# A planned attention-and-mixer kernel: z turned by overlapping twos of tiles, more buffers, shared homes for turned blocks, later projections

## The chip, the cores and the metric

One NeuronCore of a Trainium2 chip runs the whole kernel. Its engines are TensorE (PE, matmuls; PEld are its weight loads), VectorE (DVE), ScalarE (ACT), GpSimd (POOL) and SyncE (SP, which here only issues DMAs). The metric is device time in microseconds (us) of one launch; less is better.

## The reference

Eight batches of 3200 tokens; `u`, `v` have 256 columns, `z` has 64, the weights are 256 x 64 (`w_q`, `w_k`) and 256 x 256 (`w_out`). All is given and returned in float32.

```python
# gated attention
scores = matmul(z, z.transpose(0, 2, 1)) / S
attn = maximum(scores, 0.0) ** 2
x = u * matmul(attn, v)
# token mixer without softmax
wq, wk = x @ w_q, x @ w_k
W_tok = einsum('bsd,btd->bst', wq, wk) / sqrt(64)
mixed = einsum('bst,btd->bsd', W_tok, x)
out = maximum(mixed, 0.0) @ w_out
```

## The kernel before

**Tiling.** A batch's 3200 tokens are 25 tiles of 128 rows (`NT`), in seven groups: six of 512 rows and a last one of 128 (`widths`, `starts`, `LASTG`). For each group of columns `gi` the kernel forms scores against tiles `ti` of rows: one matmul of 64 x 128 by 64 x 512. Since z has 64 columns, half the rows of the array are enough for one tile; two tiles run side by side on the upper and the lower half. So z^T has to stand twice, in partitions 0 to 63 and again in 64 to 127.

**Stages.** `use_pair` (line 632) takes one of two PSUM slots, calls `scores` (242) for a pair of tiles, and gives the eviction max(., 0) times a constant to ScalarE or VectorE (`first_stage`, 262). `squares` (650) gives the square, in float16, to ScalarE or GpSimd (`second_stage`, 279); it lands in one of `NAT` = 14 buffers `at`. Scores are symmetric, so a block computed for group `gi` also serves group `gj` if it is transposed: `turn` (304) does this with a DMA transpose issued by SyncE, for groups at a distance of 1 or 2 and for the last group (`is_turned`, 212). Turned blocks live in tiles `tt1` (three), `tt2` (four) and `ttl` (eight). `second_product` (326) accumulates block times v into four PSUM banks (two halves of the group, two halves of the array). When a half is complete, `gate` (342) copies one bank on ScalarE, adds the other on VectorE and multiplies with u on GpSimd: that is `x_sb`, `NX` = 6 buffers. Later `turn_x` (380) transposes x by DMA, `projections` (397) forms queries and keys, `turn_keys` (416) transposes these, `double_keys` (426) copies them on GpSimd, `heads` (433) accumulates the small matrix keys^T x, and `mix` and `proj` (462, 485) form the output.

**z.** For the first batch, z is loaded in four pieces, doubled by casts into `zd0` and transposed on TensorE. For each later batch, `load_z` (154) loads z in float16 through GpSimd's DMA queue to `zn`; `double_z` (158) copies it twice on VectorE, so that each 128-column block of `zd` holds one tile's 64 columns two times; and `turn_z` (163) makes five DMA transposes of five blocks each into `zT`.

**What sets the order.** The program is written out by a planner. It keeps a clock for each engine with fixed costs, and at each step chooses the next piece of work for TensorE: a pair of scores, an extra (`keys`, `heads`, `mix`, `proj`) or the next step of the second product (loop at 963). SyncE's DMAs wait in `moves`, each with a time from which it may go and a due time; the earliest due goes first (`flush`, 598). A pair may be computed only when all readers of its `at` buffer have been planned and its transposes have landed (line 981). `XWAIT` (818) holds the projections back after x has been turned; `z_here` (803) holds scores of a batch until its last turn of z has landed in the plan. On the chip the engines run in the order so written, each held by semaphores.

Of the kernel before, what the change touches and what calls it, by code (L numbers as in the profile page):

```python
# [16 lines left out]
def kernel(  # L17
# [10 lines left out]
    nc = tc.nc  # L28
# [20 lines left out]
    ALPHA = C1 * float(S) * float(S)  # L49
    FINAL_SCALE = 1.0 / (8.0 * ALPHA * ALPHA * ALPHA)  # L50

    NAT = 14
    NX = 6
    NEARBY = 8
    KEEP = 4

# [6 lines left out]
    pxt = ctx.enter_context(tc.tile_pool(name="pxt", bufs=3))  # L63
# [18 lines left out]
    def top(r):  # L82
        return slice(r * dqk, (r + 1) * dqk)

    ctx.enter_context(tc.manual_schedule())

    zT, vs, us, xs, xTs, qks, ks, hacc, hss, rts, zds = ({} for _ in range(11))

    def rows(t, b):
        return t[b].rearrange("(p n) d -> p n d", n=NT)  # L90
# [6 lines left out]
    zd0 = pz.tile([P, NT, 2, dqk], FP16, tag="zd", name="zd")  # L97
    vs[0] = pv.tile([P, NT, D], FP16, tag="v_sb", name="v_sb")
    zT[0] = pzt.tile([P, S], FP16, tag="zT2", name="zT2")

    def load_first_z():
        for i, (n0, nn) in enumerate(ZCH):
# [49 lines left out]
    zdense, ztimes = {}, []  # L152

    def load_z(b):
        zdense[b] = pz.tile([P, NT, dqk], FP16, tag="zn", name="zn")
        nc.gpsimd.dma_start(out=zdense[b][:], in_=rows(z, b))

    def double_z(b, half):
        if half == 0:
            zds[b] = pz.tile([P, NT, 2, dqk], FP16, tag="zd", name="zd")  # L160
        nc.vector.tensor_copy(out=zds[b][:, :, half, :], in_=zdense[b][:])

    def turn_z(b, i):
        ztimes.append((b, i))
        if i == 0:
            zT[b] = pzt.tile([P, S], FP16, tag="zT2", name="zT2")
        nc.sync.dma_start_transpose(
            out=zT[b][:].rearrange("p (n s) -> p n s", s=P)[:, 5 * i : 5 * i + 5, :],
            in_=zds[b][:, 5 * i : 5 * i + 5, :, :].rearrange("p n a k -> p (n a k)"),
        )  # L170

    def load_u(b, gi):
        n0, nn = starts[gi] // P, widths[gi] // P
# [2 lines left out]

    wq32 = consts.tile([P, NC, dh], FP32, tag="wq32", name="wq32")
    wk32 = consts.tile([P, NC, dh], FP32, tag="wk32", name="wk32")  # L180
# [27 lines left out]


    SKIP = [(0, 2)]  # L210

    def is_turned(b, gi, gj):
        if b == 0 and (gi, gj) in SKIP:
            return False
        return gi < gj and (gj <= gi + FAR or gj == LASTG)

    def group_of(ti):
# [20 lines left out]
    NTILE = len(tiles)  # L238
    NPAIR = NTILE // 2
    made, turned = {}, {}  # L240

    def scores(p):
        assert len(ztimes) >= 5 * tiles[2 * p + 1][0] and p_chunk(p) in z_at, (p, clock, len(ztimes), z_at)
        sc = ps_tile("sc")
        for h, (b, gi, ti) in enumerate(tiles[2 * p : 2 * p + 2]):
            gs, gw = starts[gi], widths[gi]
            nc.tensor.matmul(  # L247
                out=sc[:, h, 0:gw],
                lhsT=zT[b][top(h), ts(ti, P)],
                rhs=zT[b][top(h), ds(gs, gw)],  # L250
                start=True,
                stop=True,
            )
        return sc
# [24 lines left out]
    def second_stage(p, g, ways):  # L279
        at = pat.tile([P, 2 * W], FP16, tag="at", name="at")  # L280
        at0 = 0
        parts = pieces(p)
        if len(ways) > len(parts):
            parts = [(slice(h, h + 1), parts[0][1]) for h in range(2)]
        for (hs, w), on_act in zip(parts, ways * 2):
            n = hs.stop - hs.start
            out = at[:, at0 : at0 + n * w].rearrange("p (n w) -> p n w", w=w)
            if on_act:
                nc.scalar.square(out=out, in_=g[:, hs, 0:w])  # L289
            else:  # L290
                nc.gpsimd.tensor_mul(out=out, in0=g[:, hs, 0:w], in1=g[:, hs, 0:w])  # L291
# [12 lines left out]
        def turn(b, gi, gj, n0, nn, c0, c1):  # L304
            if (b, gi, gj) not in turned:
                kind, nr, bufs = ("l", 1, 8) if gj == LASTG else (gj - gi, 4, gj - gi + 2)
                turned[b, gi, gj] = ptt.tile(
                    [P, nr, 4, P], FP16, tag=f"tt{kind}", name=f"tt{kind}", bufs=bufs
                )
# [32 lines left out]
    def gate(b, gi, half):  # L342
# [8 lines left out]
        )  # L351
        if b == last and gi >= LASTG - 2:
            if gi == LASTG - 2 and half == 0:
                spare = pz.tile([P, NT, 2, dqk], FP16, tag="zd", name="xd")
                spare = spare[:].rearrange("p n a k -> p (n a k)")
                spare = spare[:, 0 : 9 * D].rearrange("p (n d) -> p n d", d=D)
# [21 lines left out]
        make_x()  # L378

    def turn_x(b, gi):  # L380
        assert len(xTs) < 3
# [236 lines left out]
    def cold():  # L618
        return 2.0 if clock[PE] < 8.4 else 1.0

    SPLIT = 0.2
    UNTIL = 24.0

# [26 lines left out]
    def squares():  # L650
        while pending and pending[0][0] <= clock[PE] + 0.3:
# [8 lines left out]
                done = give(ACT, ready, 1.06) if on_act else give(POOL, ready, 1.9)  # L660
            for (b, gi, gj, _, nn, _, _), turn in second_stage(p, g, ways):
                n = nn * widths[gi] // P
                due = done + (4.0 if gj == gi + 1 else 9.0)
                out_of[p] = out_of.get(p, 0) + 1
                move(done + SLACK, due + SLACK, 1.28, 0.21 * n, turn, lambda t, x=(p, b, gi, gj, nn): block_landed(t, *x))
            for x in tiles[2 * p : 2 * p + 2]:
                row_at[x] = done + 0.6

# [100 lines left out]
        dma_at[0] = max(dma_at[0], clock[PE]) + takes  # L769

    Z0 = 24
    V0 = 56
    V1 = 11

    def batch_begun(b, t):
        if b + 1 < B:
            t0 = max(t + 6, Z0)
            at_time(t0, lambda: (load_z(b + 1), push(3.0)))
            for half in range(2):
                at_time(  # L780
                    t0 + 12 + 3 * half,
                    lambda half=half: (double_z(b + 1, half), give(DVE, clock[PE], 0.98)),
                )
# [18 lines left out]

    def z_here(p):
        b = tiles[2 * p + 1][0]
        return not b or z_ready.get((b, 4), 1e9) <= clock[PE]

    def group_begun(b, gi, t):
        if gi == 0:
# [6 lines left out]
    SPARE = 0.3  # L815
    BIAS = 0.2
    XDUE = 5.0
    XWAIT = 3.0
    LATE = 0.3

    last_x = []
# [1 line left out]
    def half_done(b, gi, half):  # L823
# [8 lines left out]
        if make_x:  # L832
            last_x.append(make_x)
        elif half == halves(gi)[-1]:
            n = 8 if widths[gi] == W else 2
            move(
                t + SLACK, t + XDUE, 1.28, 0.21 * n, lambda: turn_x(b, gi),
                lambda t: x_landed(t, b, gi), lambda: len(xTs) < 3,
            )

    def x_landed(t, b, gi):
# [52 lines left out]
    def acc_step():  # L894
# [6 lines left out]
        fn()  # L901
        clock[PE] += 0.1093 * cold()
        used.add(row)
        if closes:
            half_done(b, gi, half)
        return True
# [191 lines left out]
```

## Time and profile before

| what | value |
|---|---|
| three plain times | 783.07, 788.03, 788.28 us (median 788.03) |
| profiled execution | 784.44 us, of which the span from first to last instruction is 782.7 us |
| DMA transposes of squares (`tt`), of the last group (`ttl`) | 143 and 48, 4.3 and 3.7 us from issue to landing |
| DMA transposes of x, of keys, of z | 56, 53 and 35; 5.8, 4.1 and 4.8 us |
| loads of z after the first batch | 7 of 400 KB, 6.8 us |
| DMA queue of SyncE | 82.1% of the 16 DMA engines' span |

All spans, waits and counts are of the one profiled execution. Busy time of TensorE includes the filling of its pipeline: a matmul of 256 columns is shown as 269 ns, while the next may start after some 107.

### The profile page before, as it was taken

What the parts mean: (1) busy time and instruction counts of PE and PEld (TensorE: products, weight loads), DVE (VectorE), ACT (ScalarE), POOL (GpSimd) and SP (SyncE); (2) the same over time, 40 slices, a digit from 0 to 9 for tenths busy, and PEclk for the clock granted to TensorE, in tenths of its full rate; (3) what the DMA queues carried; (4) which work ended last, traced back from release to release, by engine and by line L of the source; (5) the groups of instructions that cost most, each with busy time, mean ns of one, the idle gap of its engine ahead of it and who ended that gap; (6) DMA issues with size and microseconds to landing.
All of it is one profiled execution on the core that took longest, in us unless ns stands there. A gap on an engine that the chain in (4) does not pass through costs nothing.

```text
span 782.7 us, 28343 instructions
## 1 busy us (share of the span) xinstructions
PE 769.8 (98%) x12410; PEld 663.7 (85%) x12410; DVE 503.3 (64%) x515; ACT 546.4 (70%) x663; POOL 645.1 (82%) x530
## 2 busy tenths in 40 slices
PE   7999999999999999999999999999999999999996
PEld 5899999788899878888889887998889888898784
DVE  6766556655587556786476665777567556566635
ACT  6868777668676767766677767776678676777534
POOL 7898988788889877888789889778788879888961
PEclk9999999999999999999999999999999999999999
DMA  7999999999999999999799989999999998969635
GB/s 179 143 174 170 157 181 180 165 175 206 216 174 177 211 184 189 185 212 189 180 177 174 220 173 201 168 164 217 190 188 152 183 228 166 202 127 210 142 59 213
DMA packets 306300, 140.88 MB, mean 180 GB/s; under 512 B 285056, under 2 KB 287744, under 8 KB 306176
## 3 DMA queue, kind: packets, MB, share of 16 engines
q1 hardware_dynamic: 299408, 122.90, 82.1%
q0 software_dynamic: 6624, 15.98, 15.0%
q8 instruction: 97, 1.59, 0.9%
q10 hardware_dynamic: 144, 0.20, 0.1%
q14 instruction: 27, 0.22, 0.1%
HBM read 59.64 MB, written 26.21 MB: 110 GB/s over the span
## 4 chain that ended last, share of the span: by engine, by line
PE 92%; DVE 2%; DMA 1%; ACT 1%; POOL 1%; issue 1%; DVEq 0%; SPq 0%; ACTq 0%
PE acc L332 67%; PE sc L247 13%; PE fo L493 6%; PE qk L401 3%; PE qk L438 2%; PE mx L466 1%; DVE g L273 1%; DMA v_sb<-in_v_dram 1%; POOL at L291 1%; ACT g L269 1%; ACT at L289 0%; DMA z<-in_z_dram 0%; DVE fo L516 0%; PE hd L438 0%; DVE both L349 0%
## 5 line engine op out<-in xcount | busy, mean ns | idle before, releaser
L291 POOL TENSOR_TENSOR at<-g 128x1024 f16<-128x1024 f32 (+2 forms) x252 | 457.1, 1827 | 62.4 <-DVE g L273 50.3
L332 PE MATMUL acc<-v_sb,at 64*128 64x256 f16 x7344 | 498.4, 269 | 1.2 <-DMA v_sb<-in_v_dram 0.7
L273 DVE TENSOR_SCALAR g<-sc 128x1024 f32<-128x1024 f32 (+2 forms) x320 | 372.6, 1178 | 135.3 <-PE sc L247 126.7
L332 PEld LDWEIGHTS <-at 64*128 64x128 f16 x7344 | 400.9, 94 | 55.2 <-issue 8.1
L289 ACT ACTIVATE at<-g 128x1024 f16<-128x1024 f32 (+2 forms) x230 | 228.1, 1008 | 19.2 <-DVE g L273 17.0
L269 ACT ACTIVATE g<-sc 128x1024 f32<-128x1024 f32 (+2 forms) x159 | 156.5, 986 | 67.1 <-PE sc L247 58.5
L247 PE MATMUL sc<-zT 64*128 64x512 f16 x924 | 187.6, 377 | 1.9 <-DVE g L273 0.8
L370 POOL TENSOR_TENSOR x_sb<-both,u_sb 128x512 f16<-128x512 f32 (+1 forms) x112 | 134.7, 1209 | 43.9 <-DVE both L349 43.6
L332 PE MATMUL acc<-v_sb,tt 64*128 64x256 f16 x2272 | 159.2, 269 | 0.0
L332 PEld LDWEIGHTS <-tt 64*128 64x128 f16 x2272 | 123.5, 94 | 14.3
L349 DVE TENSOR_TENSOR both<-acc,both 128x512 f32<-128x512 f32 (+1 forms) x104 | 69.7, 670 | 86.4 <-ACT both L348 73.3
L348 ACT COPY both<-acc 128x512 f32<-128x512 f32 (+1 forms) x104 | 59.0, 568 | 70.7 <-PE acc L332 66.4
L247 PEld LDWEIGHTS <-zT 64*128 64x128 f16 x924 | 60.8, 94 | 12.9 <-issue 8.9
L521 ACT ACTIVATE fo<-fo 128x1024 f32<-128x1024 f32 (+1 forms) x48 | 44.6, 930 | 24.3 <-PE fo L493 23.8
L493 PE MATMUL fo<-wo,rt 128*128 128x256 f16 x400 | 53.2, 274 | 1.3 <-ACT rt L481 0.5
L483 ACT ACTIVATE rt<-mx 128x1024 f16<-128x1024 f32 (+1 forms) x49 | 45.6, 934 | 11.5 <-PE mx L466 11.2
L414 ACT CAST qk<-qk 128x512 f16<-128x512 f32 (+1 forms) x54 | 29.4, 544 | 30.0 <-PE qk L438 24.1
L493 PEld LDWEIGHTS <-rt 128*128 128x128 f16 x400 | 34.9, 98 | 15.8 <-issue 10.9
L453 DVE TENSOR_TENSOR ha<-qk,ha 128x512 f32<-128x512 f32 x37 | 25.6, 691 | 30.7 <-ACT qk L414 30.2
L401 PE MATMUL qk<-xT_sb,wqk 64*128 64x256 f16 (+1 forms) x404 | 32.4, 265 | 0.0
L431 POOL COPY kx<-kx 128x128 f16<-128x128 f16 (+1 forms) x99 | 26.2, 294 | 5.7 <-DMA kx<-qk 5.7
L438 PE MATMUL qk<-x_sb,kx 64*128 64x256 f16 x342 | 28.4, 269 | 0.0
(45 smaller groups left out, 233.7 us busy)
## 6 DMA issues: line engine op xcount, KB each, us to landing
u_sb<-in_u_dram SPq DMA_DIRECT2D x48, 512.0 KB, 4.9
out_dram<-fo SPq DMA_DIRECT2D x47, 512.0 KB, 5.2
v_sb<-in_v_dram POOLq DMA_DIRECT2D x35, 320.0 KB, 5.5
zn<-in_z_dram POOLq DMA_DIRECT2D x7, 400.0 KB, 6.8
tt<-at SPq DMA_TRANSPOSE x143, 4.3
u_sb<-in_u_dram SPq DMA_DIRECT2D x8, 128.0 KB, 3.1
out_dram<-fo SPq DMA_DIRECT2D x8, 128.0 KB, 3.4
xT_sb<-x_sb SPq DMA_TRANSPOSE x56, 5.8
```

Of the source, the lines that this page charges most:

```text
L247: nc.tensor.matmul(out=sc[:, h, 0:gw], lhsT=zT[b][top(h), ts(ti, P)], rhs=zT[b][top(h), ds(gs, gw)], start=True, stop=True,)
L269: nc.scalar.activation(out=g[:, hs, 0:w], in_=sc[:, hs, 0:w], func=RELU, scale=GSCALE)
L273: nc.vector.tensor_scalar(out=g[:, hs, 0:w], in0=sc[:, hs, 0:w], scalar1=0.0, scalar2=GSCALE, op0=AOP.max, op1=AOP.mult,)
L289: nc.scalar.square(out=out, in_=g[:, hs, 0:w])
L291: nc.gpsimd.tensor_mul(out=out, in0=g[:, hs, 0:w], in1=g[:, hs, 0:w])
L332: nc.tensor.matmul(out=accs[half, r][:, ds((j % 2) * D, D)], lhsT=weights(b, gi, ti, j)[top(r), :], rhs=vs[b][top(r), ti, :], start=(first ...
L348: nc.scalar.copy(out=both[:, 0 : n * D], in_=accs[half, 0][:, 0 : n * D])
L349: nc.vector.tensor_add(out=both[:, 0 : n * D], in0=accs[half, 1][:, 0 : n * D], in1=both[:, 0 : n * D])
L370: nc.gpsimd.tensor_mul(out=xs[b, gi][:, 0:n, :, r, :].rearrange("p n c d -> p (n c) d"), in0=both[:, 0 : n * D].rearrange("p (m d) -> p m ...
L401: nc.tensor.matmul(out=ps[:, r, 0 : n * P], lhsT=wqk[top(r), c, :, :].rearrange("p t h -> p (t h)"), rhs=xTs[b, gi][top(r), 0:n, c, :], st ...
L483: nc.scalar.activation(out=out, in_=ps[:, 0:nr, 0 : ND * n * P], func=RELU)
L493: nc.tensor.matmul(out=banks[r][:, ds(j * D, D)], lhsT=flat[:, ds((dc * n + j) * P, P)], rhs=wo[:, dc, :], start=(dc == 0 and j == 0), sto ...
```

## The change

- z of the later batches isn't copied any more. `zn` becomes one tile of 27 blocks of 64 columns: a zero block, the 25 tiles, a zero block. A transpose of two neighbouring blocks gives 128 rows: the left tile above, the right tile below. All overlapping twos are turned (blocks 0 and 1, 1 and 2, up to 25 and 26), the even ones in two DMAs of seven and six, the odd ones likewise. In `zT` each tile then stands below in its own column block, and above one block further right, so `zT` has 128 more columns and `z_cols` shifts the upper half's reads.
- The turns may go from 14 us after the load in the plan, in steps of 7 (5 in the first batch), instead of from 18 in steps of 6 (4).
- `NAT` goes from 14 to 16, `NX` from 6 to 7, the buffers of turned x from 3 to 4 (`NXT`).
- Blocks at a distance of 1 or 2 share seven homes, which are handed out and given back in the plan; a turn without a free home waits (`has_home`). Their due time is 4 us at distance 1, 9 at 2, and 12 for the last group's farther blocks.
- `XWAIT` goes from 3 to 7.
- The first batch's doubled z, and the last batch's x, use a buffer of v; the first weights use one of the output buffers. `EXTRA` is empty.

```diff
-    NAT = 14
-    NX = 6
+    NAT = 16
+    NX = 7
+    NXT = 4
...
     def load_z(b):
-        zdense[b] = pz.tile([P, NT, dqk], FP16, tag="zn", name="zn")
-        nc.gpsimd.dma_start(out=zdense[b][:], in_=rows(z, b))
-
-    def double_z(b, half):
-        if half == 0:
-            zds[b] = pz.tile([P, NT, 2, dqk], FP16, tag="zd", name="zd")
-        nc.vector.tensor_copy(out=zds[b][:, :, half, :], in_=zdense[b][:])
+        nc.gpsimd.dma_start(out=zn[:, 1 : NT + 1, :], in_=rows(z, b))
 
     def turn_z(b, i):
+        odd, m0, m1 = ZTURNS[i]
         ztimes.append((b, i))
         if i == 0:
-            zT[b] = pzt.tile([P, S], FP16, tag="zT2", name="zT2")
+            zT[b] = pzt.tile([P, S + P], FP16, tag="zT2", name="zT2")
         nc.sync.dma_start_transpose(
-            out=zT[b][:].rearrange("p (n s) -> p n s", s=P)[:, 5 * i : 5 * i + 5, :],
-            in_=zds[b][:, 5 * i : 5 * i + 5, :, :].rearrange("p n a k -> p (n a k)"),
+            out=zT[b][:].rearrange("p (m o s) -> p o m s", o=2, s=P)[:, odd, m0:m1, :],
+            in_=zn[:, 2 * m0 + odd : 2 * m1 + odd, :].rearrange("p n k -> p (n k)"),
         )
+
+    def z_cols(b, h, at, n):
+        return zT[b][top(h), ds(at + (P if b and h == 0 else 0), n)]
...
+    NHOME = 7
+    homes, homes_free = {}, list(range(NHOME))
+
+    def has_home(b, gi, gj):
+        return gj == LASTG or (b, gi, gj) in turned or bool(homes_free)
+
+    def give_home_back(b, gj, t):
+        gi = group_of(t)
+        if (b, gi, gj) in homes and all(
+            (b, gj, starts[gi] // P + n) in used for n in range(widths[gi] // P)
+        ):
+            homes_free.append(homes.pop((b, gi, gj)))
...
-                lhsT=zT[b][top(h), ts(ti, P)],
-                rhs=zT[b][top(h), ds(gs, gw)],
+                lhsT=z_cols(b, h, ti * P, P),
+                rhs=z_cols(b, h, gs, gw),
...
-                due = done + (4.0 if gj == gi + 1 else 9.0)
+                due = done + {1: 4.0, 2: 9.0}.get(gj - gi, FARDUE)
...
-            for half in range(2):
-                at_time(
-                    t0 + 12 + 3 * half,
-                    lambda half=half: (double_z(b + 1, half), give(DVE, clock[PE], 0.98)),
-                )
-            step = 6 if b else 4
-            for i in range(5):
+            step = ZSTEP if b else ZSTEP0
+            for i, (_, m0, m1) in enumerate(ZTURNS):
                 move(
-                    t0 + 18 + step * i, t0 + 34 + step * i, 1.28, 1.05,
+                    t0 + ZWAIT + step * i, t0 + ZDUE + step * i, 1.28, 0.21 * (m1 - m0),
...
-    XWAIT = 3.0
+    XWAIT = 7.0
```

Here `ZTURNS = [(0, 0, 7), (1, 0, 7), (0, 7, 13), (1, 7, 13)]`, `ZWAIT, ZDUE, ZSTEP, ZSTEP0 = 14.0, 32.0, 7.0, 5.0` and `FARDUE = 12.0`.

More of the change, by code (lines that the diff above doesn't have):

```diff
@@ L62 @@
     pk = ctx.enter_context(tc.tile_pool(name="pk", bufs=3))
-    pxt = ctx.enter_context(tc.tile_pool(name="pxt", bufs=3))
+    pxt = ctx.enter_context(tc.tile_pool(name="pxt", bufs=NXT))
     pu = ctx.enter_context(tc.tile_pool(name="pu", bufs=2))
@@ L85 @@
     ctx.enter_context(tc.manual_schedule())
-    zT, vs, us, xs, xTs, qks, ks, hacc, hss, rts, zds = ({} for _ in range(11))
+    zT, vs, us, xs, xTs, qks, ks, hacc, hss, rts = ({} for _ in range(10))
     def rows(t, b):
@@ L96 @@
     z32 = {}
-    zd0 = pz.tile([P, NT, 2, dqk], FP16, tag="zd", name="zd")
+    zd0 = pv.tile([P, NT, 2, dqk], FP16, tag="v_sb", name="zd")
     vs[0] = pv.tile([P, NT, D], FP16, tag="v_sb", name="v_sb")
-    zT[0] = pzt.tile([P, S], FP16, tag="zT2", name="zT2")
+    zT[0] = pzt.tile([P, S + P], FP16, tag="zT2", name="zT2")
+    zn = pz.tile([P, NT + 2, dqk], FP16, tag="zn", name="zn")
     def load_first_z():
@@ L150, in load_v @@
         nc.gpsimd.dma_start(out=vs[b][:, n0 : n0 + nn, :], in_=rows(v, b)[:, n0 : n0 + nn, :])
-    zdense, ztimes = {}, []
+    ztimes = []
+    ZTURNS = [(0, 0, 7), (1, 0, 7), (0, 7, 13), (1, 7, 13)]
     def load_z(b):
-        zdense[b] = pz.tile([P, NT, dqk], FP16, tag="zn", name="zn")
-        nc.gpsimd.dma_start(out=zdense[b][:], in_=rows(z, b))
-    def double_z(b, half):
-        if half == 0:
-            zds[b] = pz.tile([P, NT, 2, dqk], FP16, tag="zd", name="zd")
-        nc.vector.tensor_copy(out=zds[b][:, :, half, :], in_=zdense[b][:])
+        nc.gpsimd.dma_start(out=zn[:, 1 : NT + 1, :], in_=rows(z, b))
     def turn_z(b, i):
+        odd, m0, m1 = ZTURNS[i]
         ztimes.append((b, i))
         if i == 0:
-            zT[b] = pzt.tile([P, S], FP16, tag="zT2", name="zT2")
+            zT[b] = pzt.tile([P, S + P], FP16, tag="zT2", name="zT2")
         nc.sync.dma_start_transpose(
-            out=zT[b][:].rearrange("p (n s) -> p n s", s=P)[:, 5 * i : 5 * i + 5, :],
-            in_=zds[b][:, 5 * i : 5 * i + 5, :, :].rearrange("p n a k -> p (n a k)"),
-        )
+            out=zT[b][:].rearrange("p (m o s) -> p o m s", o=2, s=P)[:, odd, m0:m1, :],
+            in_=zn[:, 2 * m0 + odd : 2 * m1 + odd, :].rearrange("p n k -> p (n k)"),
+        )
+    def z_cols(b, h, at, n):
+        return zT[b][top(h), ds(at + (P if b and h == 0 else 0), n)]
     def load_u(b, gi):
@@ L175, in load_u @@
         nc.sync.dma_start(out=us[b, gi][:, 0:nn, :], in_=rows(u, b)[:, n0 : n0 + nn, :])
-    wq32 = consts.tile([P, NC, dh], FP32, tag="wq32", name="wq32")
-    wk32 = consts.tile([P, NC, dh], FP32, tag="wk32", name="wk32")
+    w32s = pg.tile([P, 2, W], FP32, tag="fo", name="w32s", bufs=2)
+    w32s = w32s[:, 0, :].rearrange("p (i c h) -> p i c h", i=2, h=dh)
+    wq32, wk32 = w32s[:, 0, :, :], w32s[:, 1, :, :]
     wqk = consts.tile([P, NC, 2, dh], FP16, tag="wqk", name="wqk")
@@ L210 @@
     SKIP = [(0, 2)]
+    EXTRA = []
     def is_turned(b, gi, gj):
@@ L214, in is_turned @@
             return False
+        if b and (gi, gj) in EXTRA:
+            return True
         return gi < gj and (gj <= gi + FAR or gj == LASTG)
@@ L240 @@
     made, turned = {}, {}
+    NHOME = 7
[8 more added lines that the diff above has]
+            homes_free.append(homes.pop((b, gi, gj)))
     def scores(p):
-        assert len(ztimes) >= 5 * tiles[2 * p + 1][0] and p_chunk(p) in z_at, (p, clock, len(ztimes), z_at)
+        assert len(ztimes) >= 4 * tiles[2 * p + 1][0] and p_chunk(p) in z_at, (p, clock, len(ztimes), z_at)
         sc = ps_tile("sc")
@@ L305, in turn @@
             if (b, gi, gj) not in turned:
-                kind, nr, bufs = ("l", 1, 8) if gj == LASTG else (gj - gi, 4, gj - gi + 2)
-                turned[b, gi, gj] = ptt.tile(
-                    [P, nr, 4, P], FP16, tag=f"tt{kind}", name=f"tt{kind}", bufs=bufs
-                )
+                if gj == LASTG:
+                    tag, nr, bufs = "ttl", 1, 8
+                else:
+                    homes[b, gi, gj] = home = homes_free.pop(0)
+                    tag, nr, bufs = f"tt{home}", 4, 1
+                turned[b, gi, gj] = ptt.tile([P, nr, 4, P], FP16, tag=tag, name=tag, bufs=bufs)
             out = turned[b, gi, gj][:].rearrange("p n j t -> p (n j) t")
@@ L353, in gate @@
             if gi == LASTG - 2 and half == 0:
-                spare = pz.tile([P, NT, 2, dqk], FP16, tag="zd", name="xd")
-                spare = spare[:].rearrange("p n a k -> p (n a k)")
-                spare = spare[:, 0 : 9 * D].rearrange("p (n d) -> p n d", d=D)
+                spare = pv.tile([P, NT, D], FP16, tag="v_sb", name="xd")
                 for i in range(3):
@@ L380, in turn_x @@
     def turn_x(b, gi):
-        assert len(xTs) < 3
+        assert len(xTs) < NXT
         n = min(2, widths[gi] // P)
@@ L619, in cold @@
         return 2.0 if clock[PE] < 8.4 else 1.0
+    FARDUE = 12.0
     SPLIT = 0.2
@@ L662, in squares @@
                 n = nn * widths[gi] // P
-                due = done + (4.0 if gj == gi + 1 else 9.0)
+                due = done + {1: 4.0, 2: 9.0}.get(gj - gi, FARDUE)
                 out_of[p] = out_of.get(p, 0) + 1
-                move(done + SLACK, due + SLACK, 1.28, 0.21 * n, turn, lambda t, x=(p, b, gi, gj, nn): block_landed(t, *x))
+                move(
+                    done + SLACK, due + SLACK, 1.28, 0.21 * n, turn,
+                    lambda t, x=(p, b, gi, gj, nn): block_landed(t, *x),
+                    lambda x=(b, gi, gj): has_home(*x),
+                )
             for x in tiles[2 * p : 2 * p + 2]:
@@ L771 @@
     Z0 = 24
+    ZWAIT, ZDUE, ZSTEP, ZSTEP0 = 14.0, 32.0, 7.0, 5.0
     V0 = 56
@@ L777, in batch_begun @@
             t0 = max(t + 6, Z0)
+            if b == 0:
+                nc.gpsimd.memset(zn[:, 0 : NT + 2 : NT + 1, :], 0.0)
             at_time(t0, lambda: (load_z(b + 1), push(3.0)))
-            for half in range(2):
-                at_time(
-                    t0 + 12 + 3 * half,
-                    lambda half=half: (double_z(b + 1, half), give(DVE, clock[PE], 0.98)),
-                )
-            step = 6 if b else 4
-            for i in range(5):
+            step = ZSTEP if b else ZSTEP0
+            for i, (_, m0, m1) in enumerate(ZTURNS):
                 move(
-                    t0 + 18 + step * i, t0 + 34 + step * i, 1.28, 1.05,
+                    t0 + ZWAIT + step * i, t0 + ZDUE + step * i, 1.28, 0.21 * (m1 - m0),
                     lambda i=i: turn_z(b + 1, i),
@@ L804, in z_here @@
         b = tiles[2 * p + 1][0]
-        return not b or z_ready.get((b, 4), 1e9) <= clock[PE]
+        return not b or z_ready.get((b, 3), 1e9) <= clock[PE]
     def group_begun(b, gi, t):
@@ L837, in half_done @@
                 t + SLACK, t + XDUE, 1.28, 0.21 * n, lambda: turn_x(b, gi),
-                lambda t: x_landed(t, b, gi), lambda: len(xTs) < 3,
+                lambda t: x_landed(t, b, gi), lambda: len(xTs) < NXT,
             )
@@ L903, in acc_step @@
         used.add(row)
+        if row:
+            give_home_back(*row)
         if closes:
```

## The prediction

> **What bounds the kernel now.** I read the page first: who is busy, at which clock, and what the chain that ended last consists of.
>
> ```profile
> PE 769.8 (98%) x12410; PEld 663.7 (85%) x12410; DVE 503.3 (64%) x515; ACT 546.4 (70%) x663; POOL 645.1 (82%) x530
> ...
> PEclk9999999999999999999999999999999999999999
> ...
> PE 92%; DVE 2%; DMA 1%; ACT 1%; POOL 1%; issue 1%; DVEq 0%; SPq 0%; ACTq 0%
> ```
>
> TensorE (PE) is busy 98% of 782.7 us at full granted clock, and 92% of the closing chain is its own matmuls. The next view, busy time by stretch of the span, tells where its 12.9 idle us lie; the columns are the stretch, its length, then busy time and count of PE, PEld, DVE, ACT, POOL.
>
> ```profile
> 0.00:20.00 20.00, 15.84 (x192) 11.88 (x194) 13.20 (x18) 12.28 (x20) 14.82 (x22) 1.00 0.75 177
> 20.00:60.00 40.00, 38.96 (x635) 34.80 (x633) 28.38 (x29) 30.91 (x40) 35.64 (x29) 1.00 1.02 161
> ...
> 100.00:200.00 100.00, 99.14 (x1625) 85.36 (x1621) 60.66 (x63) 73.63 (x86) 84.85 (x72) 1.00 1.11 180
> 200.00:300.00 100.00, 100.00 (x1626) 86.92 (x1624) 67.24 (x68) 67.41 (x80) 85.07 (x72) 1.00 1.08 198
> ...
> 765.00:782.00 17.00, 11.09 (x98) 6.97 (x96) 9.46 (x11) 7.92 (x16) 1.24 (x2) 0.98 0.60 233
> ```
>
> 4.16 us are idle before 20 us and 5.91 after 765; between them the nine stretches add up to 2.13 (1.04, 0, 0.86, 0, 0, 0.12, 0, 0.11, 0). Matmul ends are modelled, so short waits can hide behind the 269 ns of a matmul. I therefore also took the spacing of matmul starts: a pair of 256-column matmuls on the two halves of the array follows the last pair after 109 to 111 ns almost always. Starts that come more than 120 ns behind the columns of the matmul before them (at 2.4 columns per ns, which 109 ns nearly is) sum to 12.5 us over the kernel; of these 3.4 us lie between 37 and 765 us. That is the whole stock that an edit in the middle can win, whatever it relieves. The waits of PE name the holders:
>
> ```profile
> PE hd L438 <- POOL kx L431: 0.9, 1, 0.9
> PE sc L247 <- DVE g L273: 0.8, 3, 0.4
> PE sc L247 <- ACT g L269: 0.8, 3, 0.3
> ...
> PE acc L332 <- DVE both L349: 0.4, 2, 0.2
> ```
>
> The columns are us in total, times, longest. The longest wait behind the start is the one at 138.5 us: heads waiting for GpSimd's doubled keys.
>
> Now the groups that the change touches (busy us, mean ns, idle before):
>
> ```profile
> L291 POOL TENSOR_TENSOR at<-g 128x1024 f16<-128x1024 f32 (+2 forms) x252 | 457.1, 1827 | 62.4 <-DVE g L273 50.3 <-issue 3.7 <-ACT g L269 3.5
> ...
> L289 ACT ACTIVATE at<-g 128x1024 f16<-128x1024 f32 (+2 forms) x230 | 228.1, 1008 | 19.2 <-DVE g L273 17.0
> ...
> L161 DVE COPY zd<-zn 128x1600 f16<-128x1600 f16 x14 | 13.7, 975 | 0.0
> ```
>
> **The change part by part.** The sum goes against the profiled execution: 784.44 us, a span of 782.7 and 1.7 around it. That is 3.6 under the median of the three plain times (788.03; they run from 783.07 to 788.28).
>
> TensorE's work. Both programs have the same matmuls on it (10,000 for the second product, 924 scores, and as many projections, heads, mixes and final products); six head matmuls only move from the combined slot to one of their own. Cost 0. Its order is the same up to matmul work that the trace of before reaches at about 35 us, and the end (last gram onward) is the same too. So the idle 4.16 at the start and 5.91 at the end stay, and only the middle is open.
>
> z. Fourteen copies of 975 ns leave VectorE: 13.7 us. VectorE idles 279.4 us of the span (782.7 - 503.3) and its rows wait mostly for PE (126.7 us behind scores), so the copies were under cover: 0 on the path, at most the 0.8 + 0.4 us in which PE waited for VectorE. The transposes go from 35 of five blocks to 28 of six or seven, 26 blocks a batch for 25. SyncE issues one in about 1.29 us, nearly the same for four blocks as for eight, so 7 x 1.29 = 9 us of its queue come free; everything behind them there (turned squares, u, x and keys) starts a little sooner. That is hidden again unless a landing is late for PE, which the waits above show nowhere but in v at the start. The first turn now follows the load of z by some 7 us of PE work in the first batch (12 to 29 in the others). A load takes a median of 6.8 us after an issue that GpSimd reaches 2 to 4 us behind the plan, and SyncE is itself some 5 us late there (median over 191 squares), so SyncE may stand about 1 us, 3 at worst, with a turned square, u and x queued behind. The square's first reader is 25 us of PE work away: 0, and 3 us if that cover were gone.
>
> When is z whole? At the tightest boundary of before the last turn was issued at 171.44 and the first score that reads it began at 177.57:
>
> ```profile
> 171.44 1.79 SPq L167 DMA_TRANSPOSE zT<-zd  x1
> ...
> 177.57 0.38 PE L247 MATMUL sc<-zT 64*128 64x512 f16 x1
> ```
>
> With the median 4.8 us to landing that left 1.4 us. In the order of the changed program the last turn stands 22.8 to 33.6 us of PE work before the first reader, against 13.9 to 24.1, and longer in six of seven boundaries (+9.0, +2.0, +4.2, +9.5, +6.3, +1.5, -0.3). So no wait is added; none was there to remove.
>
> Sixteen squares, seven x, four turned x, projections four us later. In program order the distance between the last reader of a square's buffer and its next writer grows from a 25th percentile of 7.5 to 11.4 us of PE work, and of x from a smallest 23.0 to 27.8. Neither shows as a wait of PE before. Doubled keys stand at least 3.99 us of PE work before the heads that read them, against 3.61 (3.77 at the wait of 138.5 us). I take 1.0 us back for that wait. It may be replaced by another, so 0 to 3.4 us (the whole stock) bound the gain here.
>
> Shared homes. The same seven buffers of turned blocks, now for either distance: 0. The later due time brings some turns nearer to their reader: the tenth percentile falls from 30.7 to 24.7 us of PE work, the smallest away from the start from 20.8 to 15.4, near 42 us. There SyncE lags 8 us at most and a landing takes 4.3: 12.3 is still less. Cost 0, up to 3 us if that lag doubled.
>
> ScalarE and GpSimd. With VectorE's plan lighter, 18 full squares move from GpSimd (about 1.9 us each, -34) to ScalarE (+18.1 at 1.008), while six first evictions go to VectorE. ScalarE ends near 559 us of 783, still not the bound. It copies each finished accumulator first, and a square just ahead of that copy delays it: 48 copies stand right behind a square in before's order, 54 after. Price between 0 and 6 x 1.0 us; PE reopens the bank mostly 2.3 us or more after it closes, so I take 0.
>
> A rule of the skill that bears on the copies: the Trainium skill's page "SBUF — State Buffer", section "SBUF: two separate sides", says that VectorE in a two-port mode and GpSimd take a shared port pair as an exclusive lock, so that one blocks for the whole instruction. The trace does not agree for these copies: 15 full squares on GpSimd that overlap one by over 0.3 us take a median of 1.896 us, the other 237 take 1.895. By the rule 13.7 us would return to GpSimd; by the row nothing does.
>
> Sum: 784.4 - 1.0 = 783.4 on the profile's footing, and 788.0 - 1.0 = 787.0 on the median's. Neither footing is better, so I take the middle: 785.
>
> **The rivals.**
>
> Slower, through ScalarE. The 18 squares fall just before closing accumulators, their copy is late, VectorE's sum behind it too, and PE waits to reopen the bank. For it: ScalarE is the busier by those 18, and PE does wait for L349 now (0.4 us). Against it: the planner holds evictions and squares back ahead of a close, and only six more copies have a square right before them. Price 6 us with those six, 18.1 with all; past 1% (7.8 us) it needs eight. At ten: 784.4 + 10 = 794. Chance 0.07.
>
> Slower, through a late z. If SyncE falls L us further behind, each boundary costs L less its slack; with the slack of before (4.5, 1.4, 4.8, 8.5, 8.9, 8.3, 7.9) and the shifts above, L = 10 costs about 10 us: 795. Against it: the issues get fewer. Chance 0.03. The Trainium skill ("TensorE: Matmul & The Clock Gate", HAM oscillation) adds that a PE gap over about 3.4 us halves the clock for a while; no gap here is near that (1.0 us at most behind the start), and the clock row stays at nine.
>
> Faster by over 1%. All 3.4 us go (781.0) and the runs fall on the side of the 783.07: 779.6. For it: more slack at keys, x and z. Against it: the matmuls themselves are the floor. Chance 0.07.
>
> No effect: VectorE's relief is real and off the path. That is my forecast but for 1 us, chance 0.83 with it.
>
> **How the numbers follow.** About 1% is what a measurement of this kernel can tell from no change. Range: from 779.6 (all waits of the middle gone, a fast run) to 792 (a run like the slowest, 788.3, plus two thirds of the six late copies). What is left out is most of the two slower rivals and the edge of the faster one, under 0.2. Faster 0.07, same 0.83, slower 0.10.
>
> **What would show it.** VectorE down by 13.7 less six evictions, GpSimd by 30 or more, ScalarE up by 10 to 20, PE's busy time unchanged within 2 us; the 0.9 us wait for keys gone; no wait of PE for zT; the stretches between 200 and 600 still full. I am wrong if PE's sum of idle time in the middle is above 10 us, if a wait for L349 or for a DMA leads its list, or if the spacing of the pairs itself leaves 109 ns.

## The result and the profile after

Six runs of the changed kernel gave 781.18 to 782.59 us, median 781.73; six of before beside them 783.07 to 788.28, median 787.01. The ratio is 0.9949, with a 95% interval of 0.9924 to 0.9974: faster by 0.3 to 0.8%, so a small gain, and under the bound of 1%. Ratios and intervals, here and below, are of fast runs alone: a time over 1.5% above the fastest of its kernel is left out, which concerns one of `a_x3` (799.99 us) and one of before beside it (795.81). The profiled execution took 781.65 us with a span of 779.9, against 784.44 and 782.7.

Two things differ by different amounts. From profile to profile 2.8 us are gone, from median to median 5.3. And the times of the changed kernel lie within 1.4 us of each other, where those of before spread over 5.2.

Busy time and the chain that ended last, from the page of after:

```profile
PE 768.5 (99%) x12410; PEld 666.7 (85%) x12410; DVE 494.7 (63%) x505; ACT 557.2 (71%) x673; POOL 615.0 (79%) x517
...
PE 95%; DVE 2%; ACT 1%; issue 1%; POOL 0%; DVEq 0%; POOLq 0%; ACTq 0%
```

TensorE does the same work. VectorE lost 8.6 us, GpSimd 30.1, and ScalarE took up 10.8. All three have at most 2% of the chain, so what they lost or took up can't be read off as the gain; what VectorE's copies cost is tested below (`a_cponly`). The waits of TensorE (us in total, times, longest):

```profile
PE sc L265 <- ACT g L287: 0.8, 3, 0.3
PE sc L265 <- DVE g L291: 0.6, 2, 0.4
...
PE acc L352 <- DMA v_sb<-in_v_dram: 0.4, 1, 0.4
...
PE acc L352 <- DVE both L369: 0.2, 1, 0.2
```

The 0.9 us for the doubled keys (heads, near 138 us) is gone, and nothing took its place. Starts of matmuls that come over 120 ns late sum to 1.8 us in the middle, against 3.4 before. In the same stretches as before:

```profile
0.00:20.00 20.00, 16.33 (x200) 12.62 (x202) 13.36 (x18) 12.73 (x21) 15.46 (x23) 1.00 0.78 183
20.00:60.00 40.00, 38.94 (x632) 34.83 (x629) 27.06 (x27) 31.53 (x39) 32.94 (x26) 1.00 0.99 152
...
100.00:200.00 100.00, 99.87 (x1652) 88.72 (x1649) 68.77 (x69) 70.46 (x83) 82.43 (x72) 1.00 1.13 185
200.00:300.00 100.00, 100.00 (x1642) 85.15 (x1638) 63.69 (x65) 72.41 (x86) 75.36 (x63) 1.00 1.10 195
```

The stretch from 100 to 200 us now idles 0.13 instead of 0.86. Counted along the 10,000 matmuls of the second product, after leads by 1.0 us at the 1500th, by 2.8 at the 2000th (near 155 us), and by 2.7 at the last: the gain is made before 160 us, and what follows is a draw. Of it 0.45 us lies in the first 34 us, up to where both programs have the same order on TensorE. That part is chance: a second profile of before (below) is 0.4 ahead of the first there.

### The profile page after: what moved, and what is told of

Same layout as the page of the kernel before. It is cut to its first block, busy times and chain, and to the rows that moved or that the text cites. A ratio compares the mean times of both kernels' runs of the same rounds, so it can differ in the third digit from the quotient of the medians.

```text
span 779.9 us, 28282 instructions
## 1 busy us (share of the span) xinstructions
PE 768.5 (99%) x12410; PEld 666.7 (85%) x12410; DVE 494.7 (63%) x505; ACT 557.2 (71%) x673; POOL 615.0 (79%) x517
## 4 chain that ended last, share of the span: by engine, by line
PE 95%; DVE 2%; ACT 1%; issue 1%; POOL 0%; DVEq 0%; POOLq 0%; ACTq 0%
PE acc L352 68%; PE sc L265 13%; PE fo L511 6%; PE qk L419 3%; PE qk L456 2%; PE mx L484 1%; DVE g L291 1%; ACT g L287 1%; PE warm L146 0%; ACT at L307 0%; DVE fo L534 0%; PE hd L456 0%; PE xtx L554 0%; DVE both L369 0%; POOL at L309 0%
## 5 line engine op out<-in xcount | busy, mean ns | idle before, releaser
L309 POOL TENSOR_TENSOR at<-g 128x1024 f16<-128x1024 f32 (+2 forms) x238 | 426.0, 1801 | 75.0 <-DVE g L291 57.4
L291 DVE TENSOR_SCALAR g<-sc 128x1024 f32<-128x1024 f32 (+2 forms) x324 | 378.3, 1184 | 150.9 <-PE sc L265 136.5
L307 ACT ACTIVATE at<-g 128x1024 f16<-128x1024 f32 (+2 forms) x244 | 246.0, 1020 | 23.4 <-DVE g L291 20.6
L287 ACT ACTIVATE g<-sc 128x1024 f32<-128x1024 f32 (+2 forms) x155 | 151.0, 977 | 54.8 <-PE sc L265 48.9
L352 PE MATMUL acc<-v_sb,tt 64*128 64x256 f16 x2272 | 162.7, 269 | 0.0
L352 PEld LDWEIGHTS <-tt 64*128 64x128 f16 x2272 | 125.5, 94 | 10.9
```

The lines of the kernel that those rows point to most:

```text
L287: nc.scalar.activation(out=g[:, hs, 0:w], in_=sc[:, hs, 0:w], func=RELU, scale=GSCALE)
L291: nc.vector.tensor_scalar(out=g[:, hs, 0:w], in0=sc[:, hs, 0:w], scalar1=0.0, scalar2=GSCALE, op0=AOP.max, op1=AOP.mult,)
L352: nc.tensor.matmul(out=accs[half, r][:, ds((j % 2) * D, D)], lhsT=weights(b, gi, ti, j)[top(r), :], rhs=vs[b][top(r), ti, :], start=(first ...
```

## The experiments

Three questions: what makes before's times spread, which part of the change brings the gain, and what the copies cost. Twelve kernels ran in three groups of four, each group on one chip beside 35 runs of before.

| run | median us | lowest to highest (12 runs) | ratio to before, 95% interval |
|---|---|---|---|
| b_again | 785.37 | 782.64 to 790.49 | 0.9998 (0.9975 to 1.0022) |
| z_only | 787.25 | 782.83 to 789.06 | 1.0001 (0.9979 to 1.0023) |
| a_copies | 787.20 | 785.19 to 789.71 | 1.0014 (0.9993 to 1.0034) |
| a_zlate | 787.84 | 784.11 to 790.77 | 1.0011 (0.9988 to 1.0033) |
| a_again | 781.85 | 781.53 to 785.20 | 0.9955 (0.9927 to 0.9983) |
| a_vearly | 784.29 | 783.07 to 786.60 | 0.9977 (0.9951 to 1.0004) |
| b_vearly | 784.26 | 783.18 to 791.40 | 0.9990 (0.9954 to 1.0025) |
| a_copies2 | 785.46 | 783.11 to 788.12 | 0.9980 (0.9948 to 1.0013) |
| a_vfirst | 781.70 | 781.08 to 784.30 | 0.9957 (0.9934 to 0.9980) |
| b_vfirst | 783.57 | 782.10 to 787.01 | 0.9982 (0.9958 to 1.0006) |
| a_cponly | 785.18 | 783.77 to 789.73 | 1.0004 (0.9982 to 1.0027) |
| a_x3 | 791.01 | 785.53 to 799.99 | 1.0059 (1.0028 to 1.0089) |

**Before and after once more.** `b_again` and `a_again` are the two kernels unchanged (only a comment differs).

> The kernel before once more, unchanged, with a profile of its own. Its times spread from 783.1 to 788.3 so far, those of the changed kernel only from 781.2 to 782.6. Theory A (late inputs: in most runs of before TensorE waits at a few tight places, which the first profile caught only in part): this profile differs from the first by waits of TensorE at particular places, the keys at 138 us or the first scores of a batch near 85 and 177 us; time 784 to 788, ratio 1.00. Theory B (nothing varies but the whole): the same waits within 1 us in sum, and a time difference spread evenly over the matmuls.

> The changed kernel once more, unchanged, on the same chip and beside the same runs of before as the three others. Its first times were 781.2 to 782.6. Theory V (what varies from run to run is whether the last piece of v for the second batch, read only some 11 us of TensorE work after its load, lands in time): the changed kernel has the same short distance as before (11.2 against 10.7 us), so it is not immune: 781 to 790, median 782 to 786, waits for v near 115 us in some runs. Theory S (the change itself steadies the time): 781 to 783 again, ratio 0.993 to 0.996.

Before's second profile has a span of 783.6 us. Its lag behind the first grows by 1.4 us between the 1500th and the 2000th product matmul, and from the 2500th on it is 0.92 us behind at every step to the end. So the whole does not vary; single places do, all before 160 us. It has the same keys' wait, and a new one for a square:

```profile
PE acc L332 <- POOL at L291: 0.9, 1, 0.9
PE hd L438 <- POOL kx L431: 0.8, 1, 0.8
```

The trace gives both waits one source. Before it can double a block of keys, GpSimd waits for that block's DMA transpose; from there to the doubled keys of 139.27, and so through the late square of 131.91, it has no idle time left:

```profile
128.34 0.53 POOL L431 COPY kx<-kx 128x128 f16<-128x128 f16 x2 [3.48 <-DMA kx<-qk]
...
131.91 1.89 POOL L291 TENSOR_TENSOR at<-g 128x1024 f16<-128x1024 f32 x1
...
139.27 0.24 POOL L431 COPY kx<-kx 128x64 f16<-128x64 f16 x1
```

In the first profile of before GpSimd waits 2.03 us at the same step, up to 127.27, and is then busy up to the doubled keys of 138.21. In after it does not wait there.

The second profile of after is cleaner still: 0.1 us behind the first until 115 us, then 2.55, then 2.56 to the end. One event, with no semaphore behind it; the timeline of `a_again` (start, length, engine, operation, count, idle time before and its releaser):

```profile
112.96 5.78 SPq L331 DMA_TRANSPOSE tt<-at  x1
...
117.45 0.10 PEld L352 LDWEIGHTS <-at 64*128 64x128 f16 x2 [2.49 <-issue]
117.45 0.28 PE L352 MATMUL acc<-v_sb,at 64*128 64x256 f16 x2 [2.22 <-issue]
```

"issue" means that nothing the profile shows was waited for. The trace's DMA packets say more. TensorE's program comes in 97 packets of 16 KB on queue q8: 24,820 instructions on it, so 256 to a packet, and the packets are 7.7 us apart in the median, about what 256 instructions take. Such a packet takes 1.06 us as a rule. The one at 112.62 took 3.44, and TensorE went on 1.40 us after its end. Just then SyncE needed 5.78 us to issue one transpose, where 1.29 is usual. Two more profiles have such a stop without a semaphore: `z_only` at 116.77 (2.0 us, the packet before it took 3.97 and ended 1.51 earlier) and `a_vfirst` at 125.01 (1.8 us, the packet began 11.4 us after the last one and ended 1.31 earlier). `a_vearly` has a small one, 0.2 us at 594.6; the others have none above that.

Is it the packet? Number all of TensorE's records in order of start, from 0: the stops stand before 3521, 3521 and 3777. The last is 256 further, so all three are at the same place of a packet. Laid against the instructions that way, none of some 1,300 packets in the 14 profiles ends less than 1.31 us before its first instruction starts. The median is 5.7, and the three stops have 1.40, 1.50 and 1.31. So at these places TensorE had run out of instructions. That other transfers held the packets up is likely (the view by stretches has the DMA queues at 1.45 from 112 to 116 us here, its second value from the end; 1.13 is the mean from 100 to 200 us in after), but not shown.

Both expectations were half met. After isn't immune: four of its twelve times lie between 783.2 and 785.2. But eight lie within 0.8 us of its fastest, and of before's 35 beside it only twelve lie within 1.5 us of theirs (782.34), with the rest up to 793. Its median held.

**z alone, on before.** The turns of z of the change, with 14 squares, 6 x, the old pools and `XWAIT` 3.

```diff
-        zds[b] = pz.tile(...); nc.vector.tensor_copy(out=zds[b][:, :, half, :], in_=zdense[b][:])
+        nc.gpsimd.dma_start(out=zn[:, 1 : NT + 1, :], in_=rows(z, b))
...
-            out=zT[b][...][:, 5 * i : 5 * i + 5, :], in_=zds[b][:, 5 * i : 5 * i + 5, :, :]...
+            out=zT[b][...][:, odd, m0:m1, :], in_=zn[:, 2 * m0 + odd : 2 * m1 + odd, :]...
```

> Before with only z turned in the new way: no VectorE copies, four turns from 14 us after the load; buffers, homes and the time of the projections as before. Theory Z (z's part brings the gain, by taking away a late z or the copies): ratio 0.993 to 0.996, times as narrow as those of the changed kernel. Theory X (the slack in x, keys and squares brings it): ratio 0.998 to 1.002 and a spread of 4 us or more. Theory P (any new order of the plan moves the time by some us, whatever is relieved): anything from 0.993 to 1.005, with waits at places that neither kernel has.

No gain: 1.0001. Theory Z is out; the copies' removal alone doesn't pay on before's plan. Theory P stays open: the stop at 116.77 is in neither profile of before. Its profile (787.3 us span) has that stop and a worse wait for the keys, behind 3.99 us in which GpSimd waited for the earlier block's transpose:

```profile
141.34 0.24 POOL L431 COPY kx<-kx 128x64 f16<-128x64 f16 x1
...
141.63 0.28 PE L438 MATMUL hd<-x_sb,kx 64*128 64x256 f16 x2 [2.62 <-POOL kx L431]
```

**z as late as before, on after.**

```diff
-    ZWAIT, ZDUE, ZSTEP, ZSTEP0 = 14.0, 32.0, 7.0, 5.0
+    ZWAIT, ZDUE, ZSTEP, ZSTEP0 = 18.0, 34.0, 8.0, 16.0 / 3.0
```

> The changed kernel with its four turns of z moved to where the five of before stood (from 18 us after the load, due times from 34 to 58 us). If the earlier z is what steadies the time: about 784 to 787, some of TensorE's waits at the first scores of a batch, ratio 0.998 to 1.002, spread of 3 us or more. If not: 781 to 783, ratio 0.993 to 0.996.

The time came as expected for a late z, 787.84, and the cause did not. No score waits for z. In the profile, that of the slowest of its twelve runs, TensorE waits for the last piece of v of the second batch:

```profile
116.53 4.45 PE L352 MATMUL acc<-v_sb,at 64*128 64x256 f16 x40 [5.06 <-DMA v_sb<-in_v_dram]
```

That piece is loaded 10.7 to 11.2 us of TensorE work ahead of its first reader in before and after, and 28 us or more ahead in all later batches. The load of z for the third batch follows it by 4.3 us in before, 2.9 in after and 1.1 in `a_zlate`, where the piece took 12.5 us to land instead of 7.0 and 5.3. In no profile of the study does a matmul wait for a DMA other than v's; weight loads do, for 0.2 us at most.

**v earlier.** `a_vearly` and `b_vearly` change the plan; `a_vfirst` and `b_vfirst` move only the five loads on GpSimd, 8 us, and leave every other instruction where it was.

```diff
# a_vearly on after, b_vearly on before
-    V0 = 56
-    V1 = 11
+    V0 = 46
+    V1 = 9
# a_vfirst on after, b_vfirst on before
+                if b == 0:
+                    at_time(at - 8, lambda i=i: load_v(b + 1, 5 * i, 5))
                 at_time(at, lambda i=i: v_loaded(b + 1, 5 * i, 5))
...
-        load_v(b, n0, nn)
+        if b != 1:
+            load_v(b, n0, nn)
```

> The changed kernel with the second batch's v loaded earlier: pieces from 46 us of the plan in steps of 9 instead of from 56 in steps of 11; its last piece is then read 21.7 us of TensorE work after its load instead of 11.2. Theory V: the fastest and the steadiest of all, 779 to 783, no wait for v, ratio 0.990 to 0.994. Theory S: no better than the changed kernel, and within 1 us of it.

> Before with only the second batch's v loaded earlier in the same way (last piece 23.2 us of TensorE work ahead of its reader instead of 10.7). Theory V: this small edit alone brings as much as the whole change, 781 to 784, ratio 0.993 to 0.997. Theory S: 785 to 787 as before, ratio 0.998 to 1.002, and the slow runs stay.

> The changed kernel with only the five loads of the second batch's v issued 8 us earlier; the plan books them where it did, so the order on TensorE, VectorE, ScalarE and SyncE is that of the changed kernel to the instruction, and on GpSimd only these five move. The last piece is read 16.9 us of TensorE work after its load instead of 11.2. Theory V (the runs above the floor are waits for this piece): floor 781.2 to 781.6 as before, the four slow runs of twelve gone, all within 781 to 782.5, ratio 0.992 to 0.996. If the slow runs have another source: again a third of them at 783 to 785.

> Before with the same five loads issued 8 us earlier and no other instruction moved (last piece 19.6 us of TensorE work ahead of its reader instead of 10.7). Theory V: its floor stays at 782.3 (the wait for the keys near 138 us, about 1 us, is still there) and its tail up to 793 shrinks: median 782.5 to 783.5, ratio 0.995 to 0.998. If the tail is of the keys or of z instead: median 785 to 786, ratio 0.999 to 1.001.

Theory V, that the spread is this one piece of v, fails. The re-planned pair gave 784.3 each: `a_vearly` is worse than after beside it, with new waits for keys at 612 (0.5 us) and 630 us (1.8) in its own order, and `b_vearly` still reaches 791.4. With the order held, `a_vfirst` has 781.08 as its fastest and four of twelve at 782.7 to 784.3, like `a_again`; its profile is one of these, with the stop at 125 us that no v is part of. `b_vfirst` has a median of 783.57 and a top of 787.0, where six of before's 35 lie between 788.7 and 790.8 beside it, but the interval takes in 1. Its profile has one more thing to say: the keys' wait at 138 us is gone, though nothing but those loads was moved. SyncE issued the transpose of the earlier block of keys at 118.03 instead of 121.00, it landed at 120.36 instead of 127.21, and GpSimd did not wait for it. So that wait, too, came from a late DMA. What held it up in before isn't shown; the loads of v were among the transfers ahead of it.

**The copies given back.** `a_copies` copies z in place, both sides contiguous. `a_copies2` and `a_cponly` write in the shape of before (64 columns at a step of 128); the first plans for 0.98 us each, the second for nothing, so that only VectorE's queue differs from after (and z's turns wait for the copies).

```diff
# a_copies, planned at 10 and 12 us after the load
+        nc.vector.tensor_copy(out=zn[:, 1 : NT + 1, :], in_=zn[:, 1 : NT + 1, :])
# a_copies2 and a_cponly, at 12 and 13 us
+        twos = zT[b][:, 0 : 2 * NT * dqk].rearrange("p (n a k) -> p n a k", a=2, k=dqk)
+        nc.vector.tensor_copy(out=twos[:, :, half, :], in_=zn[:, 1 : NT + 1, :])
```

> The changed kernel with 14 copies of z given back to VectorE, in place on the same tile and planned with their old cost of 0.98 us at 10 and 12 us after the load; the results are the same. If VectorE's 13.7 us were on the path: slower than the changed kernel by 5 us or more (ratio to before 1.000). If they are under cover, as predicted: within 1.5 us of the changed kernel, ratio 0.993 to 0.997, TensorE's waits within 1 us.

> The changed kernel with 14 copies of z given back to VectorE in the shape of before: 25 pieces of 64 columns written 128 apart, into the tile that the turns write afterwards, at 12 and 13 us after the load. The results are the same. If the copies as such cost time: 3 us or more above the changed kernel beside it, with waits of TensorE for VectorE's evictions at the copies. If they are under cover (975 ns each, no slower beside GpSimd): within 1.5 us of the changed kernel, and no such wait over 0.5 us.

> The changed kernel with the 14 copies on VectorE in the shape of before, at the cost of nothing in the plan: every other instruction stands where it stood, so this is the price of the copies alone. Under cover, as predicted: floor within 0.5 us of the changed kernel (781.2 to 782.0). On the path by the queue (an eviction stands 0.98 us behind a copy and TensorE waits for its slot): up to 14 x 0.98 = 13.7, and each such wait visible as TensorE waiting for an eviction of VectorE.

The clean one is `a_cponly`: its lowest time is 2.7 us above `a_vfirst`'s on the same chip (783.77 and 781.08; the latter differs from after only by those loads), its median 3.5. Beside before it stands at 1.0004: with the copies back and nothing else moved, the gain can't be seen any more. Its profile is 2.2 us behind after's, lost in four steps that end at 48, 126, 407 and 597 us; copies begin at 40.4 and 43.0, 118.8 and 120.8, 400.9 and 402.7, 592.9 and 593.8. The other three pairs cost nothing. At 404.88 TensorE waits for an eviction that stood behind the copy of 402.72:

```profile
402.72 0.98 DVE L158 COPY zT<-zn 128x1600 f16<-128x1600 f16 x1
...
403.61 1.21 DVE L295 TENSOR_SCALAR g<-sc 128x1024 f32<-128x1024 f32 x1
...
404.88 0.33 PE L423 MATMUL qk<-xT_sb,wqk 64*128 64x128 f16 x3 [0.37 <-DVE g L295]
```

The copies are not under full cover: of 13.7 us some 2 to 3 reach the path in this order. Planned for (`a_copies2`), the lowest is 1.6 above `a_again`'s and the median 3.6. `a_copies` measured something else, told at the end.

**x undone.**

```diff
-    NX = 7
-    NXT = 4
+    NX = 6
+    NXT = 3
...
-    XWAIT = 7.0
+    XWAIT = 3.0
```

> The changed kernel with the part of x undone: 6 buffers of x, 3 of turned x, projections 3 us after x as before. If the later projections take away the wait for the keys near 138 us: that wait is back, 1 to 2.8 us, floor 782.5 or more. If z and the squares do it: floor 781.2 to 781.8 as the changed kernel. Its last piece of v is read only 9.7 us of TensorE work after its load, so by theory V its tail is the longest of all: median 784 to 788.

The keys' wait did not come back in its profile, so the first theory fell. The long tail came that theory V foretold for this kernel, and longer than expected: eleven times from 785.53 to 793.46, one of 799.99. The profile is that of the lowest time, and even it waits 3 us for v at 114 us:

```profile
PE acc L352 <- DMA v_sb<-in_v_dram: 2.9, 1, 2.9
```

In this order the last piece of v is read 9.7 us of TensorE work after its load. Without the part of x the change is a loss of 0.3 to 0.9% on before; with it, a gain of 0.3 to 0.8%.

**What follows.** Shown: TensorE's matmuls are the floor. The repeats of both kernels, `z_only`, `a_zlate`, `a_vfirst` and `a_x3` differ by single stops, the large ones between 110 and 145 us. These come in through three doors, each a DMA that came late: the last v piece, a block of keys (through GpSimd), and TensorE's own instructions. Likely, but not shown, is that all three are late because transposes, v and the next z are under way at once just then. Shown too: in the plan, moves of z's turns, x's projections or v shift the orders of all queues, and with them which door is late.

Not settled: which of the change's parts keeps after's median at its floor. Two are needed in after's order: without the part of x (`a_x3`) or with the copies back (`a_cponly`) the gain is gone. Neither z's part alone (`z_only`) nor v moved ahead alone (`b_vfirst`) is enough. Fourteen squares and the old pools on after were not tried alone, nor were the later projections on before; sixteen squares or a seventh x on before do not fit into the memory beside the doubled z. No variant was shown to beat the changed kernel.

## Why the prediction was right, and where it was not

- **What bounds it.** Right. Equal work on TensorE, busy within 1.3 us of before, and full stretches from 200 to 600 us. The stock of 3.4 us in the middle was a fair ceiling for one profile: 1.6 of it went.
- **The keys.** "I take 1.0 us back for that wait": 1.0 it was, and it was not replaced. The reason given, 3.99 us of distance for 3.77, was not it, or not all: `b_vfirst` lost the same wait with its distances unchanged. GpSimd was late with the doubled keys because it had waited 2.03 us for an earlier block of keys, 11 us ahead; the prediction stopped at the last link.
- **Two footings.** "Neither footing is better, so I take the middle: 785." This is the step that failed, by 3.3 us. Three plain times over 5.2 us said that some executions held more stops than the one in the profile; I took the spread for noise of the measurement and split it. That "no effect but for 1 us" came close was in part luck, since the middle had no reason behind it. The changed kernel's median stands on its profile (781.73 and 781.65). The right reading was to ask which tight place differs from run to run. The DMA column (second value from the end), 1.02 to 1.11 in the rows shown from 20 to 300 us, was there to see, though it stands at 1.08 where nothing stopped, too.
- **The profile's footing.** There the sum, 783.4, was 1.8 us above the 781.65. Of that 0.45 is the chance in the first 34 us. `b_vfirst`, which is before without the keys' wait, is still 1.0 us behind after at the last product matmul; what makes this rest isn't traced to one place.
- **The copies at 0.** The mechanism, cover by idle time, was right for most of it and the size was off: 2.2 us of 13.7 in the profile of `a_cponly`, 2.7 between the lowest times and 3.5 between the medians, about as much as the gain itself. The bound given, 1.2 us, came from the waits for VectorE that were there, and the copies made others. An engine idle for a third of the span still has an eviction queued right behind some copies. On before's plan the same saving could not be seen (`z_only`).
- **x.** Its slack was bounded by 3.4 us, "the whole stock" of one profile. In `a_x3` the median is over 8 us above `a_vfirst`'s on the same chip. The one profile there shows 2.9 us at the last piece of v, a door that this bound did not count; the rest of the 8 us is not traced.
- **z.** No wait for z in any profile: right, and the tight 1.4 us never broke.
- **v.** Missing from the prediction. I noted a wait for v "at the start" and checked the distances of z, x, keys and turned blocks, not that of the second batch's last piece, the shortest of all behind the start.
- **ScalarE.** The rival was wrong: waits for the accumulator's sum fell from 0.4 to 0.2 us.
- **The shared port.** GpSimd's squares ran at 1.9 us beside the copies, so nothing returned to it; `a_copies` shows when the rule does hold. (The "other 237" of that comparison include 18 smaller squares; the median of the full ones is 1.895 all the same.)

## What to carry to other kernels

When repeated times of one kernel spread far wider than the effect in question, take several profiles and line them up by the count of finished matmuls: a constant gap that opens at one place is a single stop, and the place names the suspect. In a program whose order is planned, an edit of the plan can reorder all queues, so test a suspect with an edit that leaves the plan's books alone and moves one instruction. For each transfer compare the distance from issue to first reader over all batches; the outlier is the first one to suspect.

## What the runs showed of the hardware

**TensorE's instructions come by DMA and can be late.** Three stops of 1.8 to 2.4 us, each with no semaphore, each at the same place of a 16 KB instruction packet (256 instructions) and 1.3 to 1.5 us after the end of a late one, between 116 and 126 us, as told above.

**A long stop also costs the clock.** With 5.06 us without matmuls TensorE was granted half its clock from 115.5 to 122.3 us, by the trace's record of the clock (`a_zlate`; the third value from the end is the clock):

```profile
114.00:118.00 4.00, 1.47 (x15) 1.21 (x16) 0.00 (x0) 0.00 (x0) 0.81 (x1) 0.68 1.12 109
118.00:122.00 4.00, 4.00 (x36) 2.98 (x34) 1.09 (x2) 1.60 (x3) 1.26 (x1) 0.50 1.00 216
```

At the 1600th product matmul `a_zlate` was 8.1 us behind after, 5.2 of them the wait. In `z_only` 2.62 us of idling up to 141.63 were followed by 0.62 from 142 to 146 us (half the clock for 3.4 us from 142.95 on); in `a_x3` 2.9 us were followed by 1.00. The Trainium skill's page "TensorE: Matmul & The Clock Gate" (Part 1) gives an idle window of about 3.4 us, free-running. The 5.06 us agree; the 2.62 us are shorter than that window, and here the measurement decides: shorter stops can cost the clock, and do not always.

**The copy's layout decides whether VectorE and GpSimd block each other.** The contiguous copy of `a_copies`, then the strided one of before, with shortest, median and longest time in ns:

```profile
L155 DVE COPY zn<-zn x14: 567/1128/2308, 39.5 to 595.2; 128x1600 f16<-128x1600 f16 x14
```

```profile
L161 DVE COPY zd<-zn x14: 973/975/977, 40.0 to 596.4; 128x1600 f16<-128x1600 f16 x14
```

The contiguous one needs 0.57 us where it runs freely, and up to 2.3 beside GpSimd, of whose work two squares then stretch from 1.90 to 2.23 us and six x products from 1.27 to 1.61. The strided one takes 0.975 whatever GpSimd does. The exclusive lock that the Trainium skill describes ("SBUF — State Buffer", "SBUF: two separate sides") shows for the first and not for the second. The faster form was the worse neighbour.
